# Retention and two feed-forward layers on one core: a third load buffer for the second layer's weight makers, and fewer early weight loads

## The chip, the cores and the metric

The kernel runs on one core of a Trainium2 chip. The metric is the device time of one execution in microseconds (us). Engines are named as in the profile: PE is TensorE, PEld its weight loads, DVE is VectorE, ACT is ScalarE, POOL is GpSimd, SP is SyncE, which here only issues transfers.

## The reference

Float32 retention over 4 batches, 8 heads, 768 steps and head size 64, and then two feed-forward layers (512 to 2048 to 512) on the 3072 tokens that come out. The weights of both layers are drawn in float64.

```python
for t in range(S):
    state = gamma * state + einsum('bhd,bhe->bhde', k[:, :, t], v[:, :, t])
    y[:, :, t] = scale * einsum('bhd,bhde->bhe', q[:, :, t], state)
x = y as (B * S, H * D)                              # 3072 x 512
h = x @ moe_w_in;  x = (h / (1 + exp(-1.702 h))) @ moe_w_out
h = x @ moe2_w_in; out = (max(h, 0) ** 2) @ moe2_w_out
```

## The kernel before

Every product of a layer is made of three passes: an operand is split into a rounded high part and a rest, and PE adds low times high, high times high and high times low. A pass over a 128x512 tile is one matmul.

**Retention.** The tokens are cut into 24 units of 128 (`NU`). For each unit `u` the loop at lines 592 to 613 does: scores on PE (L478), the outputs of unit `u - 1` (L535, L546, L557), the masking on DVE (L487), one piece of a weight conversion (`cv_unit`), the scaling of the outputs on DVE (L570, L574), and then `cv_ahead(u)`, which may issue a load of float64 weights of the first layer (`cv_load`, L122, on POOL's queue) and scale an earlier one on ACT (L128, L129). `load_unit(u + 4)` sends for a later unit's 1 MB on SP's queue. There are five unit buffers and five buffers `raw` for the float64 weights. In `cv_ahead` the rule is one load per unit from unit 7 (`RAWU`) on, while no more than three, from unit 18 on five, are ahead of the conversions (`cv["ahead"]`).

**First layer, first four blocks of 512 tokens** (`NSTD`, loop at line 758): for each of 16 slices `f` of the hidden size `up` (12 matmuls, lines 633 to 635) and `down` two slices behind (`LOOK`; 12 matmuls, lines 664 to 666). The activation goes through ACT (`gs` L640, `gh` L641) and DVE (`gl` L645). In block 0 the rest of the first layer's weights are converted (`cv_step`). In blocks 1 to 3 `background` (line 400) runs, slice by slice, a generator that makes weights and hands it a credit of DVE time: `BG` = 4.8 us for a slice, and 0.8 us less in the fourth block from slice 5 on (line 655). Each `yield` of the generator states what its last step costs.

**The makers.** `make_first` forms the sums of the first layer's weights for Strassen-Winograd products, `make_second` those of the second layer: 32 jobs, each with a load of 512 KB float64 (`load`, L269, on ACT's queue, two buffers `raw2`), two scalings on ACT (L128 into a tile `hm`, L129 in place), the joining and rounding on DVE (L133, L138, L146), four sums (lines 369 to 373), a cast on ACT (`wq`, L375), the rest on DVE (L337) and a store of 896 KB to DRAM on POOL's queue (L338). `load(n + 2)` is queued on ACT after job `n`'s rounding. `later` puts a piece of ACT work into `acts`, and `background` issues it at its next call.

**The other blocks** (`blocks`, loop at line 1005): one block of 1024 tokens of the first layer, (0, 2), and three of the second. Each has an up stage (`up2`, eight slices `p` of seven products of six matmuls each) and a down stage (`down2`). For each product the weights, 256 KB, are fetched from DRAM on SP's queue into eight slots (`fetch`, L754). A product that goes on in an accumulator waits for ACT's copy of that accumulator (L828). In the up stage `background` is called twice per slice with 1.8 us (`BGUP`), and at slice 4 `loads` sends for the next block's tokens on POOL's queue (L679, `xb`).

All engines' orders are those in which the program is written: `tc.manual_schedule()`.

Of the kernel before, what the change touches and what calls it, by code (L numbers as in the profile page):

```python
# [10 lines left out]
F32 = mybir.dt.float32  # L11
F32R = mybir.dt.float32r
BF16 = mybir.dt.bfloat16
U32 = mybir.dt.uint32
# [5 lines left out]
P = 128  # L20
# [20 lines left out]
NSTD = 4  # L41
SLOTS = 8
EARLY = 2
BG = 4.8
CV0 = 12
RAWU = 7
# [13 lines left out]
def tile_retention_then_two_ffns(  # L60
# [29 lines left out]
    maker_ctx = ctx.enter_context(ExitStack())  # L90
# [21 lines left out]
    def cv_load():  # L112
        n = cv["load"]
        if n == len(order):
            return
        if n >= cv["b"] + cv["ahead"]:
            return
        cv["load"] += 1
        f, s = order[n]
        raw = cv_p.tile([P, 512, 2], U32, tag="raw", name=f"raw{n}", bufs=RAWS)  # L120
        src = w1[f, :, s * 512:(s + 1) * 512].bitcast(U32)
        nc.gpsimd.dma_start(out=raw, in_=src.rearrange("p (c t) -> p c t", t=2))  # L122
        cvt[n] = raw
        loaded[n] = cv["step"]

    def scale_words(hm, raw):

        nc.scalar.mul(hm, raw[:, :, 1].bitcast(F32), 2.0 ** -112)  # L128
        nc.scalar.mul(raw[:, :, 0], raw[:, :, 0], 2.0 ** -29)  # L129

    def join(out, hb):

        v.tensor_scalar(  # L133
            out=out, in0=hb, scalar1=3, scalar2=0x7FFFFFFF,
            op0=ALU.logical_shift_left, op1=ALU.bitwise_and,
        )
        yield
        v.scalar_tensor_tensor(  # L138
            out=out, in0=hb, scalar=0x80000000, in1=out, op0=ALU.bitwise_and, op1=ALU.bitwise_or
        )  # L140
        yield

    def round_up(w, raw):

        half = w.bitcast(U16).rearrange("p (c t) -> p c t", t=2)[:, :, 0]
        v.scalar_tensor_tensor(out=half, in0=half, scalar=65527.0, in1=raw[:, :, 0], op0=ALU.min, op1=ALU.add)  # L146

    def cv_a():

        n = cv["a"]  # L150
        if n == min(cv["load"], cv["b"] + 2):
            return
        cv["a"] += 1
        scale_words(cvt[n][:, :, 1].bitcast(F32), cvt[n])
# [3 lines left out]
    def cv_high():  # L158
        if held:
            w, hm, key = held[0]  # L160
            nc.scalar.copy(out=w[:, :, 0], in_=hm.rearrange("p (k c) -> p k c", c=P))
# [36 lines left out]

    def cv_ahead(u):

        if u == 18:
            cv["ahead"] = RAWS
        if u >= RAWU:
            cv_load()
        n = cv["a"]
        if n < min(cv["load"], cv["b"] + 2) and cv["step"] >= loaded[n] + 4:
            cv_a()

    def cv_step(f=None):

        cv_high()
        old = bool(held)
        if cv["b"] < cv["a"]:
            for _ in convert():
                pass
        if f is not None:
            f()
        if old:
            cv_low()
        cv_a()  # L220
        cv_load()
        cv_load()
# [25 lines left out]
    def later(fn):  # L248

        done = []  # L250

        def run():
            fn()
            done.append(True)

        acts.append(run)
        return done
# [3 lines left out]
    raws = {}  # L261
    raw_p = []

    def load(n):
        if n < len(jobs):
            m, i = jobs[n]
            raws[n] = raw_p[0].tile([P, 512, 2], U32, tag="raw", name=f"raw2_{n}")
            src = (win2, wout2)[m][i].bitcast(U32)
            nc.scalar.dma_start(out=raws[n], in_=src.rearrange("p (c t) -> p c t", t=2))  # L269

# [51 lines left out]

    def make_second():

        with tc.tile_pool(name="k2", bufs=2, side="right", reuse_waits="tile") as pool:
            hms = {}

            def scale(n):
                if n < len(jobs):
                    hm = pool.tile([P, 512], F32, tag="hm", name=f"hm2_{n}")  # L330
                    hms[n] = hm, later(lambda: scale_words(hm, raws[n]))

            def low(n, w, t, done):
                while not done:
                    yield None
                m, i = jobs[n]
                v.tensor_tensor(out=t[:, :, 1], in0=w[:, 1:8], in1=t[:, :, 0], op=ALU.subtract)  # L337
                nc.gpsimd.dma_start(  # L338
                    out=kw[1][m][i // 2][:, :, i % 2].rearrange("i p c -> p i c"),
                    in_=t.bitcast(F32).rearrange("p i h c -> p i (h c)"),  # L340
                )
                if i % 2:
                    made.add((1, m, i // 2))
                yield 1.1

            scale(0)
            last = None
            for n in range(len(jobs)):
                hm, done = hms.pop(n)
                while not done:  # L350
                    yield None
                scale(n + 1)
                raw = raws[n]
                hb = hm.bitcast(U32)
                w = pool.tile([P, 8, P], F32, tag="w", name=f"w32_{n}")
                wf = w.rearrange("p q c -> p (q c)")[:, 0:512]
                wu = wf.bitcast(U32)
                steps = join(wu, hb)
                next(steps)
                yield 0.45  # L360
                next(steps)
                yield 0.7
                round_up(wf, raw)
                later(lambda n=n: load(n + 2))
                yield 0.7
                if last is not None:
                    yield from low(*last)
                a21, a11, a12, a22, s1, s2, s3, s4 = (w[:, k] for k in range(8))
                v.tensor_tensor(out=s1, in0=a21, in1=a22, op=ALU.add)
                v.tensor_tensor(out=s3, in0=a11, in1=a21, op=ALU.subtract)  # L370
                yield 0.6
                v.tensor_tensor(out=s2, in0=s1, in1=a11, op=ALU.subtract)
                v.tensor_tensor(out=s4, in0=a12, in1=s2, op=ALU.subtract)
                t = pool.tile([P, 7, 2, P], F32R, tag="h", name=f"wq_{n}")
                done = later(lambda t=t, w=w: nc.scalar.copy(out=t[:, :, 0], in_=w[:, 1:8]))  # L375
                last = n, w, t, done
                yield 0.6
            yield from low(*last)

    def make():  # L380
        while cv["b"] < len(order):
            cv_step()
        cv_high()
        cv_low()
        cv_ctx.close()
        keep_ctx.close()
        wr_p.extend(
            wr_ctx.enter_context(tc.tile_pool(name=f"wr{i}", bufs=1, side="right", reuse_waits="tile"))
            for i in range(EARLY)
        )  # L390
        raw_p.append(maker_ctx.enter_context(
            tc.tile_pool(name="k0", bufs=2, side="right", reuse_waits="tile")
        ))
        yield from make_first()
        yield from make_second()

    maker = make()
    credit = [0.0]

    def background(us):  # L400

        credit[0] += us
        while acts:
            acts.popleft()()
        while credit[0] > 0:
            c = next(maker, None)
            if c is None:
                credit[0] = min(credit[0], 3.0)
                return
            credit[0] -= c  # L410
# [21 lines left out]
    with tc.manual_schedule():  # L432
# [195 lines left out]
        def up(n, f):  # L628
            hi, lo = weights(f, 0)
            hp = hp_p.tile([P, TB], F32, tag="h", name=f"h{n}_{f}")  # L630
            for k in range(KD):
                xh, xl = hl[n][k]
                nc.tensor.matmul(hp, lo[:, k], xh, start=(k == 0), stop=False)  # L633
                nc.tensor.matmul(hp, hi[:, k], xh, start=False, stop=False)  # L634
                nc.tensor.matmul(hp, hi[:, k], xl, start=False, stop=(k == KD - 1))  # L635
            g = g_p.tile([P, TB], F32, tag="gs", name=f"gs{n}_{f}", bufs=1)
            gh = g_p.tile([P, TB], F32R, tag="gh", name=f"gh{n}_{f}")
            gl = g_p.tile([P, TB], F32R, tag="gl", name=f"gl{n}_{f}")

            nc.scalar.activation(out=g, in_=hp, func=ACTF.Gelu_apprx_sigmoid)  # L640
            nc.scalar.copy(out=gh, in_=g)  # L641
            gs[n, f] = (gh, gl)

            def low():
                v.tensor_tensor(out=gl, in0=g, in1=gh, op=ALU.subtract)  # L645

            if n == 0 and cv["b"] < len(order):
                cv_step(low)
                if f % 4 < 3:
                    cv_step()  # L650
            else:
                low()
                if f < NF - 1:

                    background(BG if n < NSTD - 1 or f < 5 else BG - 0.8)

        def down(n, f):
            hi, lo = weights(f, 1)
# [446 lines left out]
```

## Time and profile before

| what | value |
|---|---|
| median of 3 runs (lowest, highest) | 1066.08 us (1063.63, 1067.50) |
| the profiled execution: its time, its span | 1066.25 us, 1064.5 us |
| PE busy, share of the span | 1044.9 us, 98% |
| DVE, ACT, POOL busy | 748.1, 524.2, 100.9 us |
| mean granted PE clock | 0.993 |
| HBM traffic over the span | 243 GB/s |

Times in the trace are counted from the start of the span. In a row of a waits view the columns are: engine and line that waited, what ended the wait, us in total, times, the longest. In a timeline row they are: start, duration, engine, line, operation, output from input, shape, and in brackets the idle time before it and what ended it; a row with xN is N instructions merged. In a row of a table of stretches they are: the stretch, its length, busy us of PE, PEld, DVE, ACT and POOL with the number of instructions, the granted PE clock, the share of the 16 DMA engines, GB/s. A busy PE is not a PE at its pace, since matmuls overlap: in steady work six matmuls of 128x512 start within 1.36 us.

### The profile page before, as it was taken

The numbers are of one execution on the slowest core, as the hardware profiler recorded it, in microseconds if no ns is written. First come the engines' busy times: TensorE is split into PE (matmuls) and PEld (weight loads), VectorE is DVE, ScalarE is ACT, GpSimd is POOL, SyncE is SP. The second block draws the span as 40 slices with busy tenths as digits, with TensorE's granted clock in tenths as the row PEclk, the third lists the DMA queues.
The fourth block names the chain that finished last, engine by engine and source line by source line (L and its number), as shares of the span: only waits on it lengthen the run. The fifth ranks groups of instructions, "written<-read, shape, count | busy, mean of one in ns | idle before, by whom it ended". The sixth has DMA issues, their size and how long they took to land.

```text
span 1064.5 us, 15503 instructions
## 1 busy us (share of the span) xinstructions
PE 1044.9 (98%) x5650; PEld 862.4 (81%) x5650; DVE 748.1 (70%) x1069; ACT 524.2 (49%) x858; POOL 100.9 (9%) x147
## 2 busy tenths in 40 slices
PE   9989999999999999889999999999999999999998
PEld 6878888888888888667888888888888888888886
DVE  5798997887687779744498445789355887445953
ACT  4668774444565666444546223456233454233443
POOL 3121210111111211101000100000100000000000
PEclk9999999999999999989999999999999999999999
DMA  9994989653687687888666876666876667766665
GB/s 353 407 406 141 319 279 344 237 193 139 233 270 254 231 326 268 289 288 309 206 216 194 266 258 192 191 210 213 305 204 194 188 216 236 212 193 191 208 204 162
DMA packets 106507, 259.34 MB, mean 244 GB/s; under 512 B 11200, under 2 KB 11328, under 8 KB 106176
## 3 DMA queue, kind: packets, MB, share of 16 engines
q1 hardware_dynamic: 78944, 156.64, 45.9%
q0 software_dynamic: 22304, 83.89, 22.3%
q10 hardware_dynamic: 5184, 17.83, 4.7%
q8 instruction: 45, 0.74, 0.3%
q14 instruction: 30, 0.25, 0.1%
HBM read 184.91 MB, written 73.40 MB: 243 GB/s over the span
## 4 chain that ended last, share of the span: by engine, by line
PE 90%; DMA 5%; DVE 3%; issue 1%; ACT 0%; SPq 0%; DVEq 0%
PE D L807 29%; PE X L807 16%; PE Z L807 8%; PE h L633 5%; PE h L634 5%; PE h L635 5%; PE y L666 5%; PE y L665 5%; PE y L664 5%; PE Y L807 4%; DMA unit<-qkv 2%; PE sc L478 2%; PE yp L535 2%; DMA raw<-wout 2%; DMA r<-kw 1%; PE yp L557 1%
## 5 line engine op out<-in xcount | busy, mean ns | idle before, releaser
L807 PE MATMUL D<-gx,r 128*128 128x512 f32 x1344 | 306.4, 389 | 0.0
L807 PEld LDWEIGHTS D<-gx,r 128*128 128x128 f32 x1344 | 252.0, 188 | 53.0 <-DVE gx L910 0.8
L807 PE MATMUL X<-xh,r 128*128 128x512 f32 x512 | 160.3, 395 | 6.1 <-ACT g L828 4.5
L909 ACT CAST gx<-g 128x1024 fp32r<-128x1024 f32 x112 | 116.6, 1052 | 93.0 <-PE D L807 83.4
L910 DVE TENSOR_TENSOR gx<-g,gx 128x1024 fp32r<-128x1024 f32 x112 | 136.4, 1220 | 36.9 <-ACT gx L909 36.7
L833 DVE TENSOR_TENSOR g<-Z,g 128x512 f32<-128x512 f32 x64 | 44.2, 691 | 151.0 <-ACT g L828 106.2
L828 ACT COPY g<-X 128x512 f32<-128x512 f32 x96 | 56.3, 587 | 187.7 <-PE X L807 187.7
L807 PEld LDWEIGHTS X<-xh,r 128*128 128x128 f32 x512 | 97.2, 190 | 27.9 <-ACT g L828 4.9
L666 PE MATMUL y<-gl,w 128*128 128x512 f32 x256 | 100.5, 393 | 3.0 <-DVE gl L645 3.0
L807 PE MATMUL X<-xl,r 128*128 128x512 f32 x256 | 100.6, 393 | 0.0
L665 PE MATMUL y<-gh,w 128*128 128x512 f32 x256 | 100.3, 392 | 0.0
L664 PE MATMUL y<-gh,w 128*128 128x512 f32 x256 | 100.1, 391 | 0.0
L633 PE MATMUL h<-hl,w 128*128 128x512 f32 x256 | 99.7, 389 | 0.0
L635 PE MATMUL h<-hl,w 128*128 128x512 f32 x256 | 99.6, 389 | 0.0
L634 PE MATMUL h<-hl,w 128*128 128x512 f32 x256 | 99.6, 389 | 0.0
L807 PE MATMUL Z<-xh,r 128*128 128x512 f32 x256 | 79.0, 390 | 0.8 <-DMA r<-kw 0.8
L641 ACT CAST gh<-gs 128x512 fp32r<-128x512 f32 x64 | 39.8, 622 | 71.5 <-PE y L665 70.8
L645 DVE TENSOR_TENSOR gl<-gs,gh 128x512 fp32r<-128x512 f32 x64 | 44.0, 688 | 38.8 <-ACT gh L641 38.8
L640 ACT ACTIVATE gs<-h 128x512 f32<-128x512 f32 x64 | 38.0, 594 | 46.1 <-PE h L635 37.6
L666 PEld LDWEIGHTS y<-gl,w 128*128 128x128 f32 x256 | 48.5, 189 | 13.8 <-DVE gl L645 3.8
L807 PEld LDWEIGHTS Z<-xh,r 128*128 128x128 f32 x256 | 47.9, 188 | 11.5 <-issue 1.0
L807 PEld LDWEIGHTS X<-xl,r 128*128 128x128 f32 x256 | 48.8, 191 | 10.3
(97 smaller groups left out, 1541.6 us busy)
## 6 DMA issues: line engine op xcount, KB each, us to landing
r<-kw SPq DMA_DIRECT2D x448, 256.0 KB, 2.9
kw<-wq POOLq DMA_DIRECT2D x32, 896.0 KB, 5.8
unit<-qkv SPq DMA_DIRECT2D x48, 512.0 KB, 9.5
raw<-w POOLq DMA_DIRECT2D x32, 512.0 KB, 6.6
kw<-wh POOLq DMA_DIRECT2D x16, 1024.0 KB, 4.7
kw<-w SPq DMA_DIRECT2D x16, 512.0 KB, 6.4
raw<-win ACTq DMA_DIRECT2D x16, 512.0 KB, 5.4
raw<-wout ACTq DMA_DIRECT2D x16, 512.0 KB, 4.3
```

What stands on the lines that cost most here:

```text
L633: nc.tensor.matmul(hp, lo[:, k], xh, start=(k == 0), stop=False)
L634: nc.tensor.matmul(hp, hi[:, k], xh, start=False, stop=False)
L635: nc.tensor.matmul(hp, hi[:, k], xl, start=False, stop=(k == KD - 1))
L645: v.tensor_tensor(out=gl, in0=g, in1=gh, op=ALU.subtract)
L664: nc.tensor.matmul(a, lo[:, e], gh, start=s0, stop=False)
L665: nc.tensor.matmul(a, hi[:, e], gh, start=False, stop=False)
L666: nc.tensor.matmul(a, hi[:, e], gl, start=False, stop=s1)
L807: nc.tensor.matmul(a, w, b, start=start, stop=stop, skip_group_check=True)
L828: nc.scalar.copy(out=t, in_=a)
L833: v.tensor_tensor(out=t, in0=a, in1=t, op=ALU.add)
L909: nc.scalar.copy(out=hi, in_=src)
L910: v.tensor_tensor(out=lo, in0=src, in1=hi, op=ALU.subtract)
```

## The change

Three edits. (1) In the retention one load of first layer weights is issued per two units between units 7 and 21, and the allowance of five ahead comes at unit 21, not 18. (2) `make_second` has three load buffers, each from a pool of its own, and loads three jobs ahead; the high words are scaled in place, so the tile `hm` goes and the third buffer takes its room. (3) In the fourth block the credit from slice 5 on is 1.6 us below `BG`, not 0.8.

```diff
@@ cv_ahead
-        if u == 18:
+        if u == 21:
             cv["ahead"] = RAWS
-        if u >= RAWU:
+        if u >= RAWU and (u - RAWU) % 2 == 0 or u > 21:
             cv_load()
@@ load
-            raws[n] = raw_p[0].tile([P, 512, 2], U32, tag="raw", name=f"raw2_{n}")
+            k = n % len(raw_p)
+            raws[n] = raw_p[k].tile([P, 512, 2], U32, tag="raw", name=f"raw2_{n}")
@@ make_second
-        with tc.tile_pool(name="k2", bufs=2, side="right", reuse_waits="tile") as pool:
+        with (
+            tc.tile_pool(name="k3", bufs=1, side="right", reuse_waits="tile") as third,
+            tc.tile_pool(name="k2", bufs=2, side="right", reuse_waits="tile") as pool,
+        ):
+            raw_p.append(third)
+            load(2)
             hms = {}
 
             def scale(n):
                 if n < len(jobs):
-                    hm = pool.tile([P, 512], F32, tag="hm", name=f"hm2_{n}")
+                    hm = raws[n][:, :, 1].bitcast(F32)
                     hms[n] = hm, later(lambda: scale_words(hm, raws[n]))
...
-                later(lambda n=n: load(n + 2))
+                later(lambda n=n: load(n + 3))
@@ make
-        raw_p.append(maker_ctx.enter_context(
-            tc.tile_pool(name="k0", bufs=2, side="right", reuse_waits="tile")
-        ))
+        for i in range(2):
+            raw_p.append(maker_ctx.enter_context(
+                tc.tile_pool(name=f"k0{i}", bufs=1, side="right", reuse_waits="tile")
+            ))
@@ up
-                    background(BG if n < NSTD - 1 or f < 5 else BG - 0.8)
+                    background(BG if n < NSTD - 1 or f < 5 else BG - 1.6)
```

PE's and SP's instructions stand in the same order before and after. What moves is on POOL, ACT and DVE. The change's own lines stand up to seven further down.

On POOL in the second half of the retention (`vs` is a unit's scaled values, `raw` a load of first layer weights; the number behind the name counts units or loads). Before:

```order
L497 TENSOR_TENSOR vs15_917<-unit15_752,tab_sb_127 128x512
L122 DMA raw5_1008<-w1 128x1024
L497 TENSOR_TENSOR vs18_1079<-unit18_904,tab_sb_127 128x512
L122 DMA raw6_1104<-w1 128x1024
L122 DMA raw7_1154<-w1 128x1024
L122 DMA raw8_1212<-w1 128x1024
L497 TENSOR_TENSOR vs21_1226<-unit21_1065,tab_sb_127 128x512
L122 DMA raw9_1259<-w1 128x1024
```

In the change:

```order
L504 TENSOR_TENSOR vs15_913<-unit15_752,tab_sb_127 128x512
L122 DMA raw4_947<-w1 128x1024
L122 DMA raw5_1061<-w1 128x1024
L504 TENSOR_TENSOR vs18_1079<-unit18_900,tab_sb_127 128x512
L122 DMA raw6_1150<-w1 128x1024
L504 TENSOR_TENSOR vs21_1220<-unit21_1065,tab_sb_127 128x512
L122 DMA raw7_1253<-w1 128x1024
L122 DMA raw8_1310<-w1 128x1024
L122 DMA raw9_1362<-w1 128x1024
```

Loads 7 and 8 have moved behind the work on unit 21; load 4 has moved behind that on unit 15.

On ACT at the start of the up stage of block (0, 2) (`raw2` is a load of second layer weights, `wq` the cast of a job, X an accumulator of PE that L828 copies; the first number behind `raw2` and `wq` is the job). Before:

```order
L828 COPY g11_0_4532<-X0_2_0_4560 128x512
L128 ACTIVATE hm2_28_4419<-raw2_28_4416 128x512
L129 ACTIVATE raw2_28_4416<-raw2_28_4416 128x512
L269 DMA raw2_29_4572<-wout2 128x1024
L375 CAST wq_27_4430<-w32_27_4420 128x7x128
L828 COPY g12_0_4533<-X0_2_0_4560 128x512
L835 ACTIVATE g11_0_4532<-g11_0_4532 128x512
L828 COPY g22_0_4535<-X0_2_0_4560 128x512
L128 ACTIVATE hm2_29_4575<-raw2_29_4572 128x512
L129 ACTIVATE raw2_29_4572<-raw2_29_4572 128x512
L269 DMA raw2_30_4625<-wout2 128x1024
L828 COPY g11_0_4532<-X0_2_1_4634 128x512
```

In the change:

```order
L835 COPY g11_0_4487<-X0_2_0_4515 128x512
L381 CAST wq_25_4381<-w32_25_4328 128x7x128
L128 ACTIVATE raw2_27_4325<-raw2_27_4325 128x512
L129 ACTIVATE raw2_27_4325<-raw2_27_4325 128x512
L270 DMA raw2_29_4528<-wout2 128x1024
L835 COPY g12_0_4488<-X0_2_0_4515 128x512
L842 ACTIVATE g11_0_4487<-g11_0_4487 128x512
L835 COPY g22_0_4490<-X0_2_0_4515 128x512
L381 CAST wq_26_4536<-w32_26_4382 128x7x128
L835 COPY g11_0_4487<-X0_2_1_4581 128x512
L842 ACTIVATE g22_0_4490<-g22_0_4490 128x512
L860 ACTIVATE g21_0_4489<-X0_2_0_4515 128x512
```

Here a load was issued one scaling ahead of its own scaling (29 before 29); now load 29 is issued behind scaling 27, and its own scaling comes two slices later. Two jobs more than before are left to the up stage.

On ACT where the second layer's makers begin, in slice 2 of the third block (`wh` is the last sum of `make_first`, which POOL stores to DRAM). In the change:

```order
L319 CAST wh_1_7_2958<-wt_1_7_2864 128x8x128
L270 DMA raw2_2_3008<-win2 128x1024
L647 ACTIVATE gs2_2_3023<-h2_2_3010 128x512
L648 CAST gh2_2_3024<-gs2_2_3023 128x512
L128 ACTIVATE raw2_0_2211<-raw2_0_2211 128x512
```

Before, the row of `raw2_2` stood behind the scaling of `raw2_1`. The third buffer lies where `wh` lay, and the load now waits until the store of `wh_1_7` has landed.

## Rows read from the trace of the kernel before

**Rows 1.** Waits of PE, whole span: who waited for whom, total, times, longest.

```profile
PE X L807 <- ACT g L828: 4.5, 1, 4.5
PE y L666 <- DVE gl L645: 3.0, 2, 2.0
PE sc L478 <- DVE xout L574: 1.9, 1, 1.9
PE X L807 <- DMA r<-kw: 1.6, 3, 0.8
PE Z L807 <- DMA r<-kw: 0.8, 2, 0.6
```

**Rows 2.** Chain that ended last, in order of time: start, us, what.

```profile
439.16 1.37 PE X L807 x6
...
529.58 73.61 PE D L807 x324
...
603.19 1.36 PE X L807 x6
...
682.07 73.57 PE D L807 x324
```

**Rows 3.** Timeline of PE: scores of units 16, 17, 22 and 23.

```profile
55.84 1.16 PE L478 MATMUL sc<-unit 64*128 64x128 f32 x16 [1.03 <-DMA unit<-qkv]
59.02 1.16 PE L478 MATMUL sc<-unit 64*128 64x128 f32 x16
...
75.99 1.56 PE L478 MATMUL sc<-unit 64*128 64x128 f32 x16 [1.92 <-DVE xout L574]
...
80.76 1.16 PE L478 MATMUL sc<-unit 64*128 64x128 f32 x16
```

**Rows 4.** Table of stretches of 5 us: retention, fourth block, first up stage.

```profile
75.00:80.00 5.00, 4.01 (x48) 3.81 (x48) 3.07 (x5) 2.28 (x8) 0.59 (x1) 0.66 1.01 398
...
400.00:405.00 5.00, 5.00 (x24) 4.14 (x23) 4.84 (x10) 3.37 (x6) 0.92 (x1) 1.00 0.82 286
...
450.00:455.00 5.00, 5.00 (x23) 3.76 (x21) 4.10 (x6) 2.91 (x6) 0.56 (x1) 1.00 1.03 414
...
460.00:465.00 5.00, 5.00 (x13) 3.89 (x13) 1.82 (x6) 1.15 (x3) 0.00 (x0) 0.50 0.54 177
```

**Rows 5.** Timeline of POOL: loads 6 and 7 of the retention, work on unit 21.

```profile
64.54 1.15 POOL L122 DMA_DIRECT2D raw<-w  x2
...
73.47 1.27 POOL L497 TENSOR_TENSOR vs<-unit,tab_sb 128x512 f32<-128x512 f32 x1 [3.67 <-DMA unit<-qkv]
```

**Rows 6.** Timeline of PE at the end of the fourth block.

```profile
425.69 0.39 PE L664 MATMUL y<-gh,w 128*128 128x512 f32 x1
...
431.03 0.50 PE L666 MATMUL y<-gl,w 128*128 128x512 f32 x1 [2.01 <-DVE gl L645]
...
439.00 0.61 PE L807 MATMUL X<-xh,r 128*128 128x512 f32 x2
```

**Rows 7.** Timeline of ACT and of PE in the first up stage.

```profile
457.83 0.67 ACT L128 ACTIVATE hm<-raw 128x512 f32<-128x512 f32 x1 [4.92 <-DMA raw<-wout]
...
459.56 1.22 PE L807 MATMUL X<-xh,r 128*128 128x512 f32 x2 [4.51 <-ACT g L828]
```

**Rows 8.** Tile wh: time to landing of its stores; timeline of POOL and ACT behind.

```profile
DMA to landing us min/median/max: 4.6/4.7/7.8
...
269.32 0.77 POOL L281 DMA_DIRECT2D kw<-wh  x1 [2.81 <-DVE wh L280]
...
279.01 0.60 ACT L640 ACTIVATE gs<-h 128x512 f32<-128x512 f32 x1 [0.31 <-PE h L635]
```

**Rows 9.** Groups by line and form: the scaling of the high words, in place and not.

```profile
L128 ACT ACTIVATE raw<-raw 128x512 f32<-128x512 f32 x32 | 21.8, 680 | 1.6 <-DMA raw<-w 1.6
...
L128 ACT ACTIVATE hm<-raw 128x512 f32<-128x512 f32 x32 | 21.5, 672 | 12.4 <-DMA raw<-wout 11.4 <-DMA raw<-win 0.8
```

**Rows 10.** Table of stretches of 10 us, first block.

```profile
110.00:120.00 10.00, 10.00 (x46) 8.29 (x45) 9.62 (x17) 7.69 (x15) 2.26 (x4) 1.00 0.97 336
```

## Prediction

> **What bounds the kernel now.** Read the waits of PE first [rows 1]. PE is the engine that works nearly all the time, so only the places where it stands still, or runs at its lower clock, can give anything back. They are few: ACT's copy of an accumulator (4.5 us, once), the rest of an activation on DVE (3.0 us), the wait in the retention that the view puts down to `xout` (1.9 us), and fetched weights (1.6 + 0.8 us). Everything else is PE at its pace, and no edit removes a matmul.
>
> What a wait costs is more than its length, and three further views show it. The chain in order of time gives the length of an up stage twice [rows 2]: in block (0, 2) it goes from 439.16 to 529.58, which is 90.42 us, in the next block from 603.19 to 682.07, which is 78.88 us. Both hold the same matmuls, so the first one loses 11.5 us. The timeline gives the end of the fourth block [rows 6]: from 425.69 to the first product at 439.00 there are the down parts of slices 13, 14 and 15, 36 matmuls; at six in 1.36 us [rows 2] they take 8.16 us and took 13.31, a loss of 5.15 us. And in the retention a unit takes 3.18 us (55.84 to 59.02), but unit 22 started 1.92 us late and then took 4.77 us (75.99 to 80.76) [rows 3]: 1.92 + 1.59 us, because the granted clock had fallen to 0.66 in 75 to 80 us [rows 4], which is a mean of its two levels 1.2 and 2.4 GHz. Unit 16 lost 1.03 us before.
>
> Together these three places hold 1.0 + 3.5 + 5.15 + 11.5 = 21.2 us. That is the most this change can win.
>
> **Edit 1, the retention.** Here the DMA engines are full: share 1.01, 398 GB/s [rows 4]. Loads 6 and 7 go out at 64.54 us, and load 8 stands behind them in POOL's order, all ahead of the work on unit 21 at 73.47 [rows 5]. The name on the wait of unit 22 (`xout`) belongs to work that has just ended; that the units' own data is late is my reading, from the POOL row that waits for a unit until 73.47 [rows 5]. In the change loads 7 and 8 stand behind the work on unit 21 in POOL's order, so 2 x 0.52 MB no longer share the engines with units 21 and 22: at 398 GB/s that is 2.6 us. The number of conversions in the retention stays at six, so DVE gains and loses nothing there. I take the start of unit 22 to lose its wait, and with it the slow clock: 1.92 + 1.59 = 3.5 us. Of the 1.03 us of unit 16 I count nothing: load 4 moves behind unit 15, but by unit 21 the loads 0 to 6 have gone through in either case, and PE will wait there for what it saved. From 3.5 I take off 0.5, because loads 7 to 9 now come together and can catch unit 23. **3.0 us**. Bounds: 0 (the loads catch units 22 and 23 after all) and 4.5 (all three losses).
>
> **Edit 3, the fourth block.** DVE is busy 4.84 us of 5 there [rows 4]; a slice of 24 matmuls takes PE 5.44 us, in which DVE works 5.27. That leaves no room to catch up, so DVE's part of the activation trails, and it shows when `down` follows `up` without its two slices of distance: 2.01 us for `gl` [rows 6], 3.0 in all [rows 1], and slow matmuls behind. With 0.8 us less credit DVE has about 4.5 us of work in 5.44, and the lag cannot build up. The whole loss goes: **5.1 us**. Bounds: 3.0 (the waits alone) and 5.15.
>
> Ten calls with 0.8 us less are 8 us, two jobs of some 4 us. They move into the up stage, whose DVE is busy 4.10 and 1.82 of 5 us in two stretches [rows 4], so DVE has the time, and by the new order the last job's rest comes in slice 6 or 7, still ahead of the down stage. I cost the two jobs at nothing on DVE and ACT; if that cover failed, the down stage's operands would be late next. Their two stores of 896 KB are counted below.
>
> **Edit 2, three buffers.** Take the ACT row at 457.83 [rows 7]: ACT waits 4.92 us for a load, and the copy of X queued behind it is what PE waits for until 459.56, 4.51 us. Then the clock is 0.50 in 460 to 465, which is the 1.2 GHz level: 13 matmuls there, 24 in a full stretch of the same length [rows 4]. In the new order load 29 goes out two slices ahead of its scaling, and loads 30 and 31 as well. A slice of seven products of 1.36 us takes 9.5 us [rows 2], so each has far more than the one slice that it had. So ACT should not wait there. Of the 11.5 us I leave the fetch waits of 2.4 us [rows 1]; they come mostly behind the 2 MB of the next block's tokens, which are still sent for. That makes 9.1 us. But PE then asks for weights in the 4.5 us in which it stood still: 3.3 products of 256 KB, 0.87 MB, in a stretch where the engines move 414 GB/s at a share of 1.03 [rows 4]. All of it as waits would be 2.1 us. I take 0.8 of it, since the fourth block's DVE work ends earlier and frees the slots for the first fetches earlier. **8.3 us**. Bounds: 4.9 (2.1 us of waits and as much again from a slow clock like that of 460 to 465) and 10.5.
>
> The Trainium skill, "DMA: Bandwidth & Descriptors", section "Issuing engines are not separate DMA queues", speaks against this edit: transfers from SP, ACT and POOL end up on the same 16 DMA engines and interleave, so an earlier load adds no bandwidth. The trace agrees for this stretch, with its share of 1.03; by the rule the sum for this edit would be its lower bound, 4.9 us.
>
> In place or not, a scaling costs ACT 680 or 672 ns [rows 9]: 32 x 8 ns = 0.3 us on an engine that is not the bound, nothing on the path. One wait is new: load `raw2_2` stands on ACT behind the store of `wh_1_7`, with the activation of slice 2 behind it. That store was issued at 269.32 and such stores land in 4.6 to 7.8 us [rows 8], so ACT is held until 274 or, at worst, 277. `down` of that slice comes only behind the fourth slice's `up`, at 279.01 [rows 8], and the two ACT steps that it needs take 1.2 us. I cost it at nothing, with 1 to 4 us to spare; above that PE would pay all of it.
>
> **Sum.** 3.0 + 5.1 + 8.3 = 16.4 us. The profiled execution took 1066.25 us, 1.75 more than its span and 0.17 above the median of the runs. 1066.25 - 16.4 = 1049.9 us.
>
> **Rivals.** (a) The wait changes its name: the fetches starve where ACT stood still, with edit 2 at 4.9 us. For it speak the full DMA engines [rows 4] and the two more stores, against it that PE has eight slots ahead. 1066.25 - 3.0 - 5.1 - 4.9 = 1053.2 us. The rule above gives this case.
>
> (b) The retention gains nothing, because the loads are only shifted onto units 22 and 23: 1066.25 - 13.4 = 1052.9 us. For it: ten loads have gone out by the end in both orders.
>
> (c) The change does not do what it says: the loads come out no earlier, since ACT's queue holds them behind other waits, and ACT stops PE as before. Then edit 2 gives nothing: 1058.2 us. The order speaks against it.
>
> (d) Slower. In block 0 the scaling of the first layer's weights runs ahead of the conversions by two; with the later loads by one, as ACT scales seven of the 32 before block 0 instead of eight. If each of the other 25 conversions had to wait for its two scalings, 1.36 us [rows 9], that is 34 us on a DVE that is busy 9.62 of 10 us [rows 10]; its room in some 65 us is 2.5 us, and PE would lose 31.5: 1066.25 - 16.4 + 31.5 = 1081 us. It ends slower from 0.88 us per conversion on (16.4 + 3.2 + 2.5 over 25). Against it: ACT is busy only 7.69 of 10 us there [rows 10], so a scaling is done while DVE rounds the piece before.
>
> **How the numbers follow.** Forecast 0.60, (a) 0.20, (b) 0.12, (c) 0.04, (d) 0.04. The likeliest time is 1049.9 us. The range goes from 1045.5 us (4.5, 5.15 and 10.5 us won, with half a microsecond of spread) to 1057 us, which takes in (a) and (b) together (1056.2) and leaves out (c) and (d). A measurement of this kernel can tell about 0.3% from no change, 3.2 us. All cases but (d) are faster by more than that: faster 0.94, slower 0.04, and 0.02 within, for small losses that add up.
>
> **What would show it.** Right, if in the profile after the first matmul of block 0 starts some 3 us earlier, no wait of PE for `gl` is left, the up stage of (0, 2) takes about 82 us instead of 90.4, ACT no longer waits for `raw`, and 2 to 4 us of waits for `r` remain. A stage of 85 us or more with waits for `r` above 4 us is (a); an unchanged start of block 0 is (b). Wrong altogether, if PE has idle time in block 0 behind DVE, or in the third block behind the load `raw2_2`.

## The result and the profile after

The changed kernel takes 1051.31 us (median of 6 runs, 1050.24 to 1054.99); the kernel before, run beside it, 1065.39 us. The ratio is 0.9874 with a 95% interval of 0.9858 to 0.9889. The forecast was 1049.9 us with a range of 1045.5 to 1057.0 us. The profiled execution has a span of 1049.6 us, 14.9 less than before.

Where these 14.9 us come from is read from PE's timeline, cut at four places: the first matmul of block 0 (`h`), the first of the 36 `y` matmuls that end the fourth block, the first product of block (0, 2) (`X`), and the first `D` product behind its up stage. The chain [rows 2] puts the last two cuts 0.16 us later each, which changes no length.

| stretch (us) | before | after | gain | forecast |
|---|---|---|---|---|
| start of the span to the first `h` | 85.56 | 83.56 | 2.00 | 3.0 |
| to the last `y` group | 340.13 | 341.18 | -1.05 | 0 |
| end of the fourth block | 13.31 | 8.16 | 5.15 | 5.1 |
| up stage of (0, 2) | 90.42 | 81.60 | 8.82 | 8.3 |
| rest | 535.08 | 535.10 | 0 | 0 |

The waits of PE after the change (engine and line, what ended the wait, us in total, times, longest):

```profile
PE sc L485 <- DMA unit<-qkv: 2.3, 4, 0.8
PE warm L464 <- DVE warm_sb L453: 1.2, 1, 1.2
PE Z L814 <- DMA r<-kw: 0.7, 2, 0.4
PE sc L485 <- DVE w L166: 0.5, 1, 0.5
PE X L814 <- DMA r<-kw: 0.4, 1, 0.4
PE X L814 <- ACT raw L129: 0.4, 1, 0.4
PE h L640 <- DVE w L166: 0.2, 1, 0.2
```

Against [rows 1], the wait for ACT's copy, the wait for `gl` and the wait put down to `xout` are gone, and the waits for fetched weights (`r`) are 1.1 instead of 2.4 us. New are small waits for converted weights on DVE (`w`), and one of 0.4 us before a product at 481.16 us, which the view puts down to a scaling (L129) on ACT. PE's timeline shows units 21, 22 and 23 of the retention, 3.18 us apart, which answer to [rows 3], the first matmul of block 0, and a wait at its end:

```profile
72.41 1.16 PE L485 MATMUL sc<-unit 64*128 64x128 f32 x16 [0.55 <-DMA unit<-qkv]
75.58 1.16 PE L485 MATMUL sc<-unit 64*128 64x128 f32 x16
78.76 1.16 PE L485 MATMUL sc<-unit 64*128 64x128 f32 x16
...
83.56 0.50 PE L640 MATMUL h<-hl,w 128*128 128x512 f32 x1
...
160.72 0.50 PE L640 MATMUL h<-hl,w 128*128 128x512 f32 x1 [0.24 <-DVE w L166]
```

The up stage in the chain, which answers to [rows 2]:

```profile
433.06 1.36 PE X L814 x6
...
514.66 73.61 PE D L814 x324
```

And the loads of the second layer's makers and their scalings on ACT, which answer to the first row of [rows 7]: no scaling (L128) of this stretch waits for a load (L270) now. The loads shown are 30 and 31, the scalings are those of the pieces 29 and 30: load 30 now has 20 us before its scaling.

```profile
444.26 0.34 ACTq L270 DMA_DIRECT2D raw<-wout  x1
454.83 0.67 ACT L128 ACTIVATE raw<-raw 128x512 f32<-128x512 f32 x1
...
460.37 0.33 ACTq L270 DMA_DIRECT2D raw<-wout  x1
464.35 0.69 ACT L128 ACTIVATE raw<-raw 128x512 f32<-128x512 f32 x1
```

So three stages moved about as forecast; the retention gained a third less, and block 0 lost 1.05 us. Whether each edit did what the forecast gave it is another question, and the experiments answer it otherwise.

### The profile page after: what moved, and what is told of

Its sections match the earlier page's. It is cut to its first block, busy times and chain, and to the rows that moved or that the text cites. A ratio compares the mean times of both kernels' runs of the same rounds, so it can differ in the third digit from the quotient of the medians.

```text
span 1049.6 us, 15546 instructions
## 1 busy us (share of the span) xinstructions
PE 1039.5 (99%) x5650; PEld 858.3 (82%) x5650; DVE 746.7 (71%) x1069; ACT 523.7 (50%) x858; POOL 99.2 (9%) x147
## 4 chain that ended last, share of the span: by engine, by line
PE 82%; DMA 2%; DVE 0%; issue 0%
PE D L814 29%; PE X L814 16%; PE Z L814 8%; PE y L671 4%; PE y L672 4%; PE y L673 4%; PE h L640 4%; PE h L641 4%; PE h L642 4%; PE Y L814 4%; DMA r<-kw 2%; DVE o L951 0%
## 5 line engine op out<-in xcount | busy, mean ns | idle before, releaser
L814 PE MATMUL X<-xh,r 128*128 128x512 f32 x512 | 157.8, 390 | 0.8 <-DMA r<-kw 0.4
L640 PEld LDWEIGHTS h<-hl,w 128*128 128x128 f32 x256 | 48.1, 188 | 11.4 <-DVE w L166 1.2
L814 PEld LDWEIGHTS Z<-xh,r 128*128 128x128 f32 x256 | 47.9, 188 | 11.3 <-DVE w L138 0.8
L642 PEld LDWEIGHTS h<-hl,w 128*128 128x128 f32 x256 | 48.1, 188 | 10.1
```

The source lines that it names most:

```text
L814: nc.tensor.matmul(a, w, b, start=start, stop=stop, skip_group_check=True)
```

## The experiments

The theory was that of the prediction: three edits at three separate places, whose gains add. Its rival: the edits lean on one another. Each kernel was timed beside the kernel before, whose medians were 1064.7 to 1065.3 us. The stretches are those of the table above, from each kernel's own profile, so from one execution each. The profiled execution of the kernel before, 1066.25 us, is 0.9 to 1.5 us above these medians, and gains read by stages come out larger by as much than those of the medians.

| kernel | median, us | ratio to before | first `h` | to last `y` | end of fourth | up stage |
|---|---|---|---|---|---|---|
| e1_loads | 1063.95 | 0.9987 [0.9973, 1.0] | 83.78 | 341.54 | 15.53 | 87.65 |
| e2_buffers | 1059.17 | 0.9949 [0.9933, 0.9964] | 87.07 | 340.14 | 13.56 | 81.51 |
| e3_fourth | 1054.39 | 0.9909 [0.9889, 0.9929] | 85.65 | 340.17 | 8.16 | 83.41 |
| e4_no_loads | 1054.11 | 0.9901 [0.9882, 0.9919] | 87.07 | 340.18 | 8.15 | 81.31 |
| e5_lead | 1050.54 | 0.9867 [0.9855, 0.9880] | 84.08 | 340.15 | 8.16 | 81.59 |
| e6_two | 1055.54 | 0.9916 [0.9902, 0.9930] | 85.94 | 341.21 | 8.16 | 84.35 |
| e7_tokens | 1052.52 | 0.9887 [0.9873, 0.9901] | 83.75 | 341.20 | 8.16 | 80.29 |
| e8_dense | 1052.65 | 0.9887 [0.9873, 0.9901] | 84.70 | 340.18 | 8.16 | 81.67 |
| e9_space | 1055.86 | 0.9909 [0.9894, 0.9923] | 85.45 | 340.13 | 11.75 | 81.58 |
| e10_half | 1059.05 | 0.9947 [0.9933, 0.9961] | 86.19 | 340.13 | 13.60 | 84.01 |
| e11_both | 1050.57 | 0.9867 [0.9852, 0.9882] | 85.90 | 340.17 | 8.40 | 80.94 |
| e12_two_spaced | 1050.46 | 0.9873 [0.9851, 0.9894] | 82.75 | 340.13 | 8.16 | 80.73 |

### One edit at a time

The kernel before with the first edit, and the second:

```diff
-        if u == 18:
+        if u == 21:
...
-        if u >= RAWU:
+        if u >= RAWU and (u - RAWU) % 2 == 0 or u > 21:
```

> The kernel before with the first edit alone (fewer and later loads in the retention). Separate places: block 0 starts 2.0 us earlier (first matmul at 83.6 instead of 85.56 us), and block 0 loses 1.0 us on DVE, as in the changed kernel; the later stages are untouched (end of the fourth block 13.3 us, up stage of (0, 2) 90.4 us). Net 1 us: 1064.4 us, within 0.3% of before. Rival, that the edits lean on one another: block 0 keeps the whole 2.0 us, 1063.4 us, or loses it all, 1065.4 us.

```diff
...
+            raw_p.append(third)
+            load(2)
...
-                    hm = pool.tile([P, 512], F32, tag="hm", name=f"hm2_{n}")
+                    hm = raws[n][:, :, 1].bitcast(F32)
...
-                later(lambda n=n: load(n + 2))
+                later(lambda n=n: load(n + 3))
...
```

> The kernel before with the second edit alone (three load buffers, scaled in place). Separate places: the up stage of (0, 2) falls from 90.4 to 82 us, the end of the fourth block stays at 13.3 us with its wait for gl: 1065.4 - 8.8 = 1056.6 us. Rival, that the fewer jobs in the fourth block are what relieves the up stage: up stage 86 us or more, 1061 us or more.

The third edit alone, and the change without the first:

```diff
-                    background(BG if n < NSTD - 1 or f < 5 else BG - 0.8)
+                    background(BG if n < NSTD - 1 or f < 5 else BG - 1.6)
```

> The kernel before with the third edit alone (less making in the fourth block, two load buffers). Separate places: the end of the fourth block takes 8.2 instead of 13.3 us, the up stage stays at 90.4 us: 1060.3 us. Rival, that the edits lean on one another: the two jobs that move into the up stage bring ACT two more waits for loads there, 4 to 5 us each with a slow clock behind them, so that the up stage takes 95 to 100 us and the kernel gains nothing: 1065 to 1070 us.

```diff
-        if u == 21:
+        if u == 18:
...
-        if u >= RAWU and (u - RAWU) % 2 == 0 or u > 21:
+        if u >= RAWU:
```

> The changed kernel with the loads of the retention as before (second and third edit together). Separate places: block 0 starts at 85.56 us and loses nothing, 1051.3 + 1.0 = 1052.3 us. Rival, that the retention gives the full 2.0 us and the loss in block 0 has another cause: 1053.3 us, with the 1.0 us still lost in block 0.

Edit 1 came out as expected in sum: 0.9 us in the median, at the edge of what can be told from nothing. The two stages behind it, which it does not touch, moved by 2 to 3 us against each other (15.53 and 87.65 us, together 103.2; before 103.7). PE's wait for ACT's copy is 3.1 us in this kernel and 4.5 us in the kernel before, with the same order in this stage, so the length of a stage can differ by 2 to 3 us from one profile to the next. Edit 2 did in its stage what was expected (81.51 us), with the fourth block unchanged; its median gained 5.7 and not 8.8 us. Of the 3.1 us between, 1.5 are a later start of block 0, as in e4_no_loads, though the retention's code is that of before; its cause is not found. Another 1.4 are the distance of the profiled execution of before to the median of its runs in this round.

Edit 3 fits neither theory. Alone, with two buffers, it gains 10.5 us in the median and 12.0 us between the profiles: the 5.15 us of its own place and 7.0 of the 11.5 us that the up stage lost. Nothing is left there of ACT's copy among PE's waits. The three medians alone add up to 17.1 us, the change gained 14.1. So the gains overlap, and the up stage shows where: edit 2 alone takes 8.9 us out of it and edit 3 alone 7.0, of 11.5 us that it had to lose. Behind edit 3, the three buffers take it from 83.41 to 81.31 us (e3_fourth to e4_no_loads), and the median from 1054.39 to 1054.11. e4_no_loads came out above both of its cases: block 0 loses nothing in it (340.18 us), as the first has it, but starts at 87.07 us. Put on top of the other two, edit 1 takes the median from 1054.11 to 1051.31 us, more than the 0.9 us that it gives alone, though the intervals of these two overlap.

How can less making in the fourth block relieve the up stage? The kernel before, ACT's timeline: load 30 goes out together with the scaling of piece 29, which had waited 2.51 us, and is itself waited for, 4.92 us [rows 7].

```profile
440.57 0.34 ACTq L269 DMA_DIRECT2D raw<-wout  x1
...
449.36 0.66 ACT L128 ACTIVATE hm<-raw 128x512 f32<-128x512 f32 x1 [2.51 <-DMA raw<-wout]
449.37 0.33 ACTq L269 DMA_DIRECT2D raw<-wout  x1
```

The two loads took 8.8 and 8.5 us to their scalings. With the third edit, in e3_fourth, the same two pieces stand differently:

```profile
446.09 0.33 ACTq L269 DMA_DIRECT2D raw<-wout  x1
...
456.06 0.67 ACT L128 ACTIVATE hm<-raw 128x512 f32<-128x512 f32 x1
...
461.60 0.33 ACTq L269 DMA_DIRECT2D raw<-wout  x1
...
468.01 0.68 ACT L128 ACTIVATE hm<-raw 128x512 f32<-128x512 f32 x1 [2.32 <-DMA raw<-wout]
```

Load 29 has 10 us before its scaling, so load 30 is not sent late. It is still scaled close behind its issue, and ACT still waits, 2.32 us. But the copy of X behind that scaling, which PE needs, starts at 469.17 us, 0.9 us after its product's last matmul (468.30); in the kernel before it started at 458.95 us, 5.25 us after (453.70). The credit taken out of the fourth block shifted the makers against the slices of the up stage, and that alone broke up the pair. New theory: PE stops for ACT when two loads in a row stand close ahead of their scalings, and a third buffer is one way of several to set them apart.

### The distance between a load and its scaling

Four kernels test it. Two buffers in the changed kernel, then the kernel before with other credits in the fourth block, by which the order on ACT changes:

```diff
...
-            raw_p.append(third)
-            load(2)
...
-                later(lambda n=n: load(n + 3))
+                later(lambda n=n: load(n + 2))
```

> The changed kernel with in-place scaling but two load buffers, each load two pieces ahead instead of three. If the third buffer is what frees ACT: ACT waits 4 to 5 us for loads in the up stage of (0, 2) again, which takes 90 to 95 us: 1060 to 1064 us. If the shift of two jobs out of the fourth block, or the scaling in place, does it: up stage 82 us, 1051 to 1052 us.

```diff
-                    background(BG if n < NSTD - 1 or f < 5 else BG - 0.8)
+                    background(BG if n < NSTD - 1 or f < 5 else BG - 1.4)
```

> The kernel before (two load buffers, loads of the retention as before) with 1.4 us instead of 0.8 or 1.6 us less credit in the fourth block. The order on ACT then has at least two copies between each load and its scaling in the up stage of (0, 2). If what stopped PE was the closeness of two loads and their scalings, two buffers do as well as three: up stage 81.5 to 82.5 us, end of the fourth block 8.2 us, 1053.5 us. If the third buffer gives something that spacing can't: up stage 83.4 us or more as with the third edit alone, 1054.5 us or more.

```diff
-                    background(BG if n < NSTD - 1 or f < 5 else BG - 0.8)
+                    background(BG if n < NSTD - 1 or f < 5 else BG - 1.0)
```

> The kernel before with 1.0 us instead of 0.8 us less credit in the fourth block. The first scaling (piece 29) still follows one half slice after its load, the second (piece 30) now has two copies and an activation more in front of it. If it takes two late scalings in a row to stop PE: ACT's first wait of 2.5 us stays, the one of 4.9 us is gone, PE does not wait for ACT, up stage 82 to 84 us. If each late scaling stops PE by itself: PE waits 2 us or more for ACT, up stage 86 us or more. The end of the fourth block: between 8.2 and 13.3 us, as 2 of 8 us less are made there. 1057 us by the first, 1061 us by the second.

e6_two lies between its two cases: 84.35 us, with waits of ACT of 3.11 and 1.35 us, of which PE saw 0.9, and 1055.54 us in all. So the third buffer's part behind edit 3 is 2.1 to 2.75 us (83.41 and 84.35 against 81.31 and 81.60). PE does not wait for ACT's copy in e3_fourth, and 0.9 us in e6_two. Most of what PE still stands in these two kernels is waits for fetched weights, 2.7 us in the up stage of e3_fourth and 2.0 us in that of e6_two, against 1.1 us after the change. The longest in e3_fourth:

```profile
482.59 0.74 PE L807 MATMUL X<-xh,r 128*128 128x512 f32 x2 [1.62 <-DMA r<-kw]
```

How the buffer shortens these is not shown; two-buffer kernels can have less of them too (0.8 us in e9_space, 0.5 in e12_two_spaced). In ACT's order, e10_half went as the theory has it: the first wait is there, the second is not,

```profile
450.31 0.66 ACT L128 ACTIVATE hm<-raw 128x512 f32<-128x512 f32 x1 [2.35 <-DMA raw<-wout]
...
458.71 0.67 ACT L128 ACTIVATE hm<-raw 128x512 f32<-128x512 f32 x1
```

and PE does not wait for ACT in the up stage. That takes 84.01 us, at the upper edge of what was expected, with 3.2 us of waits for fetched weights. The end of its fourth block, 13.60 us, lies outside the expected 8.2 to 13.3, and the median, 1059.05 us, between the two cases. In e9_space every load has at least two copies between it and its scaling, and two buffers reach 81.58 us, what three reach, though ACT waits once for 1.66 us. Its median, 1055.86 us, falls in the second case, but not by the up stage: the end of the fourth block took 11.75 instead of the expected 8.2 us. The rhythm of `gl` on DVE goes with it. In the kernel before it is 5.56 us per slice, above the 5.44 us of PE's 24 matmuls, so DVE falls back by 0.12 us a slice:

```profile
413.62 0.68 DVE L645 TENSOR_TENSOR gl<-gs,gh 128x512 fp32r<-128x512 f32 x1
419.18 0.69 DVE L645 TENSOR_TENSOR gl<-gs,gh 128x512 fp32r<-128x512 f32 x1
```

Over the last eight `gl` of the block it is a mean of 5.09 us in e9_space ((432.80 - 397.17) / 7) and 4.80 us in the changed kernel ((428.61 - 395.03) / 7). DVE is busy throughout in all of them up to 425 us (4.83 of 5 us in 400 to 405 us after the change). I read this as an old lag: what counts is how much of it is worked off by the end. At 1.0 us less, in e10_half, the rhythm is 5.56 us still up to 425.11 us, so whole steps of a job seem to move, not microseconds.

The last kernel puts both together, with the two buffers of before:

```diff
-BGUP = 1.8
+BGUP = 1.6
...
-                    background(BG if n < NSTD - 1 or f < 5 else BG - 0.8)
+                    background(BG if n < NSTD - 1 or f < 5 else BG - 1.6)
```

with the first edit and the double `cv_a()` of e5_lead below.

> The kernel before with the first and third edit and the scaling lead of two, but with its two load buffers; in their place 1.6 instead of 1.8 us of credit per half slice of the up stage, by which at least two copies stand between each load and its scaling on ACT. If spacing does what the third buffer does: end of the fourth block 8.2 us, up stage 81.5 us, no wait of PE for ACT, 1050.5 us as the changed kernel with the lead of two. If the third buffer gives something of its own: up stage 83.4 to 84.4 us as with two buffers and the third edit, 1052.5 to 1053.5 us.

Up stage 80.73 us, no wait of PE for ACT, 1050.46 us: spacing does here all that the third buffer does. Its waits of PE:

```profile
PE sc L479 <- DMA unit<-qkv: 2.1, 4, 0.7
PE warm L458 <- DVE warm_sb L447: 1.2, 1, 1.2
PE X L808 <- DMA r<-kw: 0.5, 2, 0.4
PE sc L479 <- DVE w L166: 0.5, 1, 0.5
PE Z L808 <- DMA r<-kw: 0.2, 1, 0.2
```

### The microsecond lost in block 0, and the retention

```diff
             cv_low()
+        cv_a()
         cv_a()
         cv_load()
```

> The changed kernel; in block 0 a step may scale twice, so that the scalings run ahead of the conversions by two from the second step on, as in the kernel before. If the 1.05 us lost in block 0 come from the scaling lead of one: PE's wait of 0.24 us for converted weights at 160 us is gone, block 0 is some 1 us shorter, 1050.3 us. If they come from the later loads themselves: as the changed kernel, 1051.3 us, and the scalings then wait for their loads on ACT.

```diff
-        if u >= RAWU and (u - RAWU) % 2 == 0 or u > 21:
+        if u >= RAWU:
             cv_load()
```

> The changed kernel; in the retention a load may go out with every unit from the seventh on, as before, and only the wider limit of five stays at unit 21. If the two late loads were what held units 21 and 22: unit 21 starts at 70.8 us as before and units 22 and 23 follow without a wait, so block 0 starts at 82.0 us and not at 83.6: 1049.7 us. If the spacing of the loads is what gives the 2.0 us: a wait before unit 16 and one before unit 22 come back, block 0 starts at 85 us or later, 1052.5 us.

Block 0 and what follows take 340.13 to 340.18 us in every kernel that scales two pieces ahead there, and 341.18 to 341.54 us in the four that scale one ahead (after, e1_loads, e6_two, e7_tokens). e8_dense belongs to the first: its denser loads have let eight pieces be scaled before block 0 instead of seven. So the scaling lead is the cause. The table of stretches shows it on DVE (the third busy number). The changed kernel:

```profile
104.00:124.00 20.00, 20.00 (x90) 16.48 (x89) 18.52 (x31) 15.46 (x28) 3.86 (x8) 1.00 0.86 283
```

The same stretch of e5_lead:

```profile
104.00:124.00 20.00, 20.00 (x90) 16.57 (x89) 19.32 (x32) 15.87 (x30) 4.85 (x9) 1.00 0.86 283
```

With a lead of one, DVE works 18.52 of 20 us, with two 19.32: it stands some 0.8 us more in each 20 us, and PE sees the end of it at 160.72 us. But DVE does not wait there for a scaling to end. A conversion begins on DVE with L133 and needs the scaling of its piece by ACT. In the changed kernel, one scaling and two starts:

```profile
109.20 0.67 ACT L128 ACTIVATE raw<-raw 128x512 f32<-128x512 f32 x1
...
109.76 0.43 DVE L133 TENSOR_SCALAR hm<-raw 128x512 uint32<-128x512 uint32 x1
...
112.44 0.43 DVE L133 TENSOR_SCALAR hm<-raw 128x512 uint32<-128x512 uint32 x1
```

And e5_lead:

```profile
109.77 0.43 DVE L133 TENSOR_SCALAR hm<-raw 128x512 uint32<-128x512 uint32 x1
...
112.32 0.43 DVE L133 TENSOR_SCALAR hm<-raw 128x512 uint32<-128x512 uint32 x1
```

The scaling at 109.20 us is that of the piece converted from 112.44 us, and had ended 2.6 us before; from the conversion at 91.24 us on, each scaling has ended at least 1.1 us before it is needed. Yet it is 2.68 us from one start to the next instead of 2.55: DVE pauses 0.08 us before L133 and 0.10 us before L146, instead of 0.03 and 0.04 us. Over 25 conversions that is some 3 us of DVE. What lengthens the pauses is not shown. PE's wait at 160 us is gone in e5_lead, and the stage gives its 1.03 us back; the median, 1050.54 us, is 0.8 us lower than that of the change, with overlapping intervals.

Of the retention, e8_dense settles a part. Its block 0 starts at 84.70 us, between the expected 82.0 and 85, and its median is 1052.65 us. Its unit 22 still waits, and here the view names the unit's own data, which the prediction had put forward as its reading:

```profile
76.73 1.16 PE L485 MATMUL sc<-unit 64*128 64x128 f32 x16 [1.55 <-DMA unit<-qkv]
```

With the old loads PE waits 1.85 to 1.92 us before unit 22 in all six kernels, the kernel before among them; with the new loads, in none of seven. So the first edit does take that wait away, and the wider limit at unit 21 alone does not. In one of the seven, e6_two, a wait of 1.73 us stands before unit 21 instead. The starts of block 0 scatter: 82.75 to 85.94 us over the seven kernels with the new loads (mean 84.25), 85.45 to 87.07 us over the six with the old ones (mean 86.17). By these means the first edit is worth 1.9 us there.

### The waits for weights that are left

```diff
-                if p == NQ // 2:
+                if p == NQ:
                     loads()
```

> The changed kernel; the next block's tokens (2 MB) are loaded at the end of each up stage instead of its middle. If the waits for fetched weights that are left in the up stage of (0, 2) come from the tokens: those at 481 and 483 us go (0.7 us) and the two at 443 and 446 us stay, 1050.5 us. Rival, that the makers' stores alone fill the DMA engines: the waits stay, 1051.3 us, or the tokens come late in the down stage and it is slower, 1053 us.

Then, on top of e5_lead, in two halves:

```diff
-                if p == NQ // 2:
+                if p in (NQ // 2, NQ - 2):
                     loads()
...
-                    gen[0] = x_operands(*x_loads(*blocks[k + 1]))
...
+                    got.append(load_block(f"xb{nl}_{nn}_{t}", (xkept, ykept)[nl][2 * nn + t]))
+                    if t == 1:
+                        gen[0] = x_operands(*got)
```

> The changed kernel with the scaling lead of two in block 0, and with the next block's tokens loaded in two halves of 1 MB, the first in the middle of the up stage and the second two slices later. If the bunch of 2 MB makes the fetches late wherever it stands: the waits for weights behind it go (0.3 to 1.1 us), none appears in the down stage, up stage 80.5 us, 1049.6 us. If it is the makers' stores that make them late: up stage 81.6 us as with the lead alone, 1050.5 us.

With the tokens at its end the up stage takes 80.29 us, 1.3 less, with two waits where the down stage begins; the median is 1052.52 us. PE's timeline of e7_tokens:

```profile
513.40 0.97 PE L814 MATMUL D<-gx,r 128*128 128x512 f32 x3 [0.68 <-DMA r<-kw]
515.38 29.99 PE L814 MATMUL D<-gx,r 128*128 128x512 f32 x131 [1.01 <-DMA r<-kw]
```

The loads were issued at 501.69 us there and at 468.78 us in the changed kernel: both times PE is short of weights 12 to 14 us later, so the waits belong to the load of the tokens and move with it. In halves, the down stage has no wait, but one of 0.99 us stays in the up stage (80.94 us), 12 us behind the first half of 1 MB, and 1050.57 us is no gain over e5_lead. So it does not take the whole 2 MB. Neither place is a gain that can be measured.

## Why the prediction was right, and where it was not

**The total** was right (1049.9 against 1051.3 us), and so were the three stages that it named. But it put the gain of the up stage down to one edit, where either of two brings most of it, and two of its terms were off. That the total still came out is in part luck: the stall in the up stage could go only once, whichever edit took it away.

**Edit 3** was forecast at 5.1 us and gives 5.15 at its place. The failing step is "I cost the two jobs at nothing on DVE and ACT": by itself the shift gains 7.0 us in the up stage. I counted how much work moves and not where, within a slice, each load and scaling then stands. The reason given for 5.1 us was also loose: DVE has no free time up to 425 us of the fourth block after the change either (4.83 of 5 us busy); its slices of 4.80 us in the mean are shorter than PE's 5.44.

**Edit 2** was forecast at 8.3 us. Alone it takes 8.9 us out of the stage, and the mechanism, a load sent two slices ahead, is confirmed by ACT's timeline. The 2 to 4 us of waits for fetched weights that were to remain came to 1.1 us. Behind edit 3 it is worth 2.1 to 2.75 us of the stage. The sum came out because the same stall was counted once, under this edit. Had edit 3 been forecast alone, I would have said 1061 us, and it takes 1054.4.

**Rival (a)** and its page: the Trainium skill, "DMA: Bandwidth & Descriptors", section "Issuing engines are not separate DMA queues", has it that transfers of all issuing engines run on the same 16 DMA engines and interleave. The prediction drew from it that an earlier load adds no bandwidth, and that the fetches would starve. In single stretches the engines are full, before the change (450 to 455 us, [rows 4]) and after it:

```profile
440.00:445.00 5.00, 4.62 (x21) 3.52 (x20) 2.83 (x5) 4.08 (x7) 0.00 (x0) 1.00 1.04 410
```

But over the whole up stage their share was 0.83 before (283 GB/s) and is 0.94 after (331 GB/s). So the stage as a whole had bandwidth left, and the fetch waits fell. What ACT was short of was the time between one load and its use.

**Edit 1** was mis-sized: 3.0 us against 2.0 in the profile and 1.9 in the means. Its 3.5 us for unit 22 did come back: it has no wait and no slow clock now. The step that failed is that unit 21 would come as before. It starts at 72.41 us; in the kernel before:

```profile
70.82 1.16 PE L478 MATMUL sc<-unit 64*128 64x128 f32 x16
```

Over the kernels (without e8_dense) unit 21 starts at 72.0 us in the mean with the old loads and at 72.9 with the new ones. Why stays open. The DMA engines moved fewer bytes earlier in the changed kernel, but that does not go with the edit. 30 to 40 us of the kernel before:

```profile
30.00:40.00 10.00, 9.59 (x194) 8.47 (x195) 5.58 (x9) 5.08 (x20) 1.58 (x2) 1.00 1.03 409
```

The changed kernel:

```profile
30.00:40.00 10.00, 10.00 (x212) 8.97 (x208) 6.29 (x10) 5.37 (x20) 2.11 (x3) 1.00 1.00 381
```

With the old loads the rate is 374 GB/s in e4_no_loads and 363 in e2_buffers, and with the new ones 408 in e12_two_spaced. The slow clock, 1.59 of the 3.5 us, is no sure gain either: behind the wait before unit 22 it came in three of the six kernels with the old loads.

The 1.05 us in block 0 were priced at nothing in the forecast. Rival (d) has the place right, block 0 with a scaling lead of one, and the price and the mechanism wrong: DVE does not wait 1.36 us for the scalings of each conversion, but loses 0.13 us per conversion with the scalings done. The sign named for it, PE idle in block 0 behind DVE, is there in small, with 0.24 us.

**ACT behind the store of `wh_1_7`** went as forecast [rows 8]: held until 274.42 us, and PE did not see it.

```profile
274.42 0.33 ACTq L270 DMA_DIRECT2D raw<-win  x1
274.80 0.60 ACT L647 ACTIVATE gs<-h 128x512 f32<-128x512 f32 x1 [8.14 <-issue]
```

## What to carry to other kernels

A stage that loses time by one cause is not several gains: when two edits both reach it, price each with the other already made. Of work that is moved, look where in the order its loads and their first use come to stand, not only at how much moves. Where a load is waited for, try first to put more work between its issue and its use in the queue; here two buffers with more distance did as well as three.

## What was not expected of the hardware

The same 512 KB load takes a median of 4.8 us to land over all 16 of its kind in the changed kernel:

```profile
raw<-wout ACTq DMA_DIRECT2D x16, 512.0 KB, 4.8
```

But it takes 6.4 to 11.3 us in this up stage where ACT's waits show its landing (8.8 and 8.5 us before, 6.4 and 11.3 in e3_fourth). So a distance of 10 us between a load and its scaling is not always enough there. Load 31 of e3_fourth, which went out as the next block's tokens were sent for:

```profile
471.48 0.35 ACTq L269 DMA_DIRECT2D raw<-wout  x1
...
482.79 0.68 ACT L128 ACTIVATE hm<-raw 128x512 f32<-128x512 f32 x1 [1.19 <-DMA raw<-wout]
```

A wait of PE of nearly the same length did and did not bring the lower clock. Before unit 22 it stood 1.92 us, and the granted clock was 0.66 in that stretch [rows 3, 4]; in e4_no_loads 1.86 us, and 0.78 and 0.88 in the two stretches; in e2_buffers 1.87 us, and 1.00 in both:

```profile
75.00:80.00 5.00, 3.13 (x66) 2.83 (x64) 3.85 (x4) 0.99 (x2) 1.93 (x2) 1.00 1.03 406
80.00:85.00 5.00, 5.00 (x108) 4.45 (x109) 4.37 (x6) 4.27 (x15) 0.00 (x0) 1.00 0.65 256
```

In the other three kernels with the old loads the wait is 1.85 to 1.89 us; e3_fourth and e9_space show 1.00 in both stretches, e10_half 0.71 and 0.95. What decides between them is not shown here.
